# Last routing of a soft mixture of experts: logits and maximum in two parts, and a new order of the copies around them

## The chip, the core and the metric

The kernel runs on one core of a Trainium2 chip. The metric is the device time of one execution in microseconds (us). Engines are named as the profile does: PE is TensorE's matmuls and PEld its weight loads, DVE is VectorE, ACT ScalarE, POOL GpSimd, SP SyncE, which issues all the DMAs. PSUM has eight banks; the program names them 0 to 7.

## The reference

Three stages follow each other: attention in chunks of 32 queries, a dense feed-forward layer (`_moe_ref`), and a soft mixture of experts (`_moe2_ref`), in which the change lies:

```python
def _moe2_ref(x, phi, w1, w2):          # x: 3072 x 512, phi: 512 x 32 (8 experts x 4 slots)
    logits = x @ phi
    d = logits - logits.max(0, keepdims=True)
    d = np.exp(d)
    d /= d.sum(0, keepdims=True) + 1e-09
    slot_input = d.T @ x
    ...
    for e in range(E):
        h = np.maximum(slot_input[e] @ w1[e], 0.0)
        slot_out[e] = h @ w2[e]
    ...
    c = logits - logits.max(1, keepdims=True)
    c = np.exp(c)
    c /= c.sum(1, keepdims=True) + 1e-09
    return (c @ slot_out).astype(np.float32)
```

`d` is normalised over all tokens, so the slot inputs, and with them the experts, need every token. `c` is normalised over the slots of one token.

## The kernel before

The 3072 tokens go through attention and the dense layer in seven blocks (`BLOCKS`, 256 to 512 tokens). `emit_h` and `emit_y` are the dense layer's matmuls; the outputs of a block collect in PSUM as `ps_y`. `route` then does the mixture's first half for a block in steps 0 to 7: y out of PSUM, transposes of y (`ps_yt`, `yT`), logits (`ps_l`, `lp`), the logits summed over four partial groups (`ps_r`, by the 0/1 matrix `sel`), a maximum over the tokens of the block (`nm`, the negated maximum, joined with that of the blocks before), Exp (`dl`, with its sum `sb`), and from its transposes `d` the block's share of the slot inputs (`ps_a`), which is added to `acc` with the factor `al` for the changed maximum. `s_run` is the running sum. It is an online softmax over tokens.

The last block (L, 512 tokens, four y tiles) has its route written out by hand, since nothing of the dense layer is left to hide it. The code runs under a manual schedule: every engine executes its instructions in the order in which they are written, and each waits for what it reads, or for the former users of the place that it writes. For PSUM, such a wait goes by the bank. The order of the last route is (lines 666 to 716): y tile 3 out of PSUM, half by ACT and half by DVE (L666, L667); the first `c_turn`; four transposes of tile 3 (L671); the logits of 384 and of 128 tokens (L679), both behind the transposes, copied to `lp` by ACT and by DVE; a `c_turn`; the sums (L687), into one bank; `route(L, 4)` with the maximum (L427), Exp (L431), two `c_turn` and two keep-warm matmuls between, the transposes `ps_d` (L442), and a copy of 32 partitions of `ps_r` to `dl[32:64]` (L444) and `s_run` (L448); `d` (L454); a `c_turn`; the reciprocal `rs` and the normalised selector `seln` (L694 to L697); `ps_a` (L469) and `acc` (L476) in two halves; the transposes of `dl[32:64]` for the combine weights (L702); keep-warm matmuls; `ps_si`, the slot inputs (L706); a keep-warm matmul; and the copies to `siz` (L709), which the experts read.

`c_turn(t0, b, eng)` is work of another branch: four PE transposes of the combine weights of tokens 128 t0 and on into bank `b` (L501), and their copy back to `c4` by `eng` ("a" is ACT, L179; "v" is DVE, L181). Only the combine at the kernel's end reads it. `keep_warm(n, b)` is n matmuls (L175) into bank `b`, which nobody reads.

Behind it, `expert1` (L725, `ps_e`) and `expert2` (L757, `ps_o`) run over weights that SP loads in 512 KB pieces (`ew`); `to_hT` (L750) transposes the hidden rows between the two. The last `c_turn` stands behind the first `to_hT`. `slot_out` sums the slots' outputs (`ps_so`, `so`), `combine` multiplies them with the combine weights (`ps_f`, L787), copies to `ob` and writes to memory.

Of the kernel before, what the change touches and what calls it, by code (L numbers as in the profile page):

```python
# [7 lines left out]
F32 = mybir.dt.float32  # L8
# [3 lines left out]
ACTF = mybir.ActivationFunctionType  # L12
ALU = mybir.AluOpType
# [42 lines left out]
def attn_moe_softmoe_kernel(  # L56
# [12 lines left out]
    nc = tc.nc  # L69
# [312 lines left out]
    def route(j, s, between=None):  # L382
# [11 lines left out]
        elif s in (1, 2):  # L394
            y = rt[j, "y"]
            if s == 1:
                rt[j, "yT"] = st_tile(1, [128, 4, n], F32, "yT")
            yT = rt[j, "yT"]
            for c in (3,) if s == 1 else (0, 1, 2):
                pt = mbank([128, n], "ps_yt")  # L400
                for t in range(nt):
                    nc.tensor.transpose(pt[:, 128 * t:128 * t + 128], y[:, t, 128 * c:128 * c + 128], ident)  # L402
                if c % 2:
                    nc.vector.tensor_copy(out=yT[:, c], in_=pt)
                else:
                    nc.scalar.activation(out=yT[:, c], in_=pt, func=ACTF.Copy)
        elif s == 3:
            yT = rt.pop((j, "yT"))
            pl = mbank([128, n], "ps_l")
            for c in range(4):  # L410
                nc.tensor.matmul(  # L411
                    pl[32 * c:32 * c + 32], phi_sb[:, c], yT[:, c], start=True, stop=True, tile_position=(0, 32 * c)
                )
            lp = rt[j, "lp"] = [sm_p.tile([128, n], F32R, tag=tag, name=tag, bufs=1) for tag in ("lp", "ll")]
            nc.scalar.activation(out=lp[0], in_=pl, func=ACTF.Copy)
            nc.vector.tensor_tensor(out=lp[1], in0=pl, in1=lp[0].bitcast(F32), op=ALU.subtract)
        elif s == 4:
            pr = rt.pop((j, "pr"), None)
            if pr is None:
                lp = rt.pop((j, "lp"))  # L420
                pr = mbank([128, n], "ps_r")
                for m, x in enumerate(lp):
                    nc.tensor.matmul(pr, selr, x, start=(m == 0), stop=(m == len(lp) - 1))
            dl = sm_p.tile([128, n], F32, tag="lp", name="dl", bufs=1)
            sb = sm_p.tile([128, 1], F32, tag="sb", name="sb")
            nm = sm_p.tile([128, 1], F32, tag="nm", name="nm")
            nc.vector.tensor_reduce(out=nm, in_=pr, axis=AX.X, op=ALU.max, negate=True)  # L427
            if j > 0:
                al = sm_p.tile([128, 1], F32, tag="al", name="al")
                nc.vector.tensor_tensor(out=nm, in0=nm, in1=rt["nm"], op=ALU.min)  # L430
            nc.scalar.activation(out=dl, in_=pr, func=ACTF.Exp, bias=nm, accum_out=sb)  # L431
            if j > 0:
                nc.vector.tensor_tensor(out=al, in0=nm, in1=rt["nm"], op=ALU.subtract)
                nc.scalar.activation(out=al, in_=al, func=ACTF.Exp)
                rt[j, "al"] = al
            rt["nm"] = nm
            if between:
                between()
            if j == NB - 1:
                pd = mbank([128, nt, 32], "ps_d")  # L440
                for t in range(nt):
                    nc.tensor.transpose(pd[:, t], dl[0:32, 128 * t:128 * t + 128], ident[0:32, 0:32])  # L442
                rt["pd"] = pd
            nc.vector.tensor_copy(out=dl[32:64], in_=pr[32:64])  # L444
            if j == 0:
                nc.vector.tensor_copy(out=s_run, in_=sb)
            else:
                nc.vector.scalar_tensor_tensor(out=s_run, in0=s_run, scalar=al, in1=sb, op0=ALU.mult, op1=ALU.add)  # L448
            rt[j, "dl"] = dl
        elif s == 5:  # L450
            dl = rt[j, "dl"]
            d = sm_p.tile([128, nt, 32], F32, tag="d", name="d")
            if j == NB - 1:
                nc.scalar.activation(out=d, in_=rt["pd"], func=ACTF.Copy)  # L454
            else:
                pd = mbank([128, nt, 64], "ps_d")
                for t in range(nt):
                    nc.tensor.transpose(pd[:, t], dl[0:64, 128 * t:128 * t + 128], ident[0:64, 0:64])
                nc.scalar.activation(out=d, in_=pd[:, :, 0:32], func=ACTF.Copy)
                slot_scores(j, pd[:, :, 32:64])  # L460
            rt[j, "d"] = d
        elif s == 6:
            y, d = rt.pop((j, "y")), rt.pop((j, "d"))
            m = 32 * nt
            cut = (0, 256, 512) if j == NB - 1 else (0, 512)
            for lo, hi in zip(cut, cut[1:]):
                pa = mbank([128, hi - lo], "ps_a")
                for t in range(nt):
                    nc.tensor.matmul(  # L469
                        pa[32 * t:32 * t + 32], d[:, t], y[:, t, lo:hi], start=True, stop=True, tile_position=(0, 32 * t)  # L470
                    )
                if j == 0:
                    nc.vector.memset(acc, 0.0)
                    nc.vector.tensor_copy(out=acc[0:m], in_=pa[0:m])
                else:
                    nc.vector.scalar_tensor_tensor(  # L476
                        out=acc[0:m, lo:hi], in0=acc[0:m, lo:hi], scalar=rt[j, "al"][0:m], in1=pa[0:m],
                        op0=ALU.mult, op1=ALU.add,
                    )
        else:  # L480
            cs = call[:, d0:d0 + nt, :]
            cm = sm_p.tile([128, nt, 1], F32, tag="cs", name="cs")
            nc.scalar.activation(out=cs, in_=cs, func=ACTF.Exp)
            nc.vector.tensor_reduce(out=cm, in_=cs, axis=AX.X, op=ALU.add)
            nc.vector.tensor_scalar(out=cm, in0=cm, scalar1=1e-9, scalar2=None, op0=ALU.add)
            nc.vector.reciprocal(out=cm, in_=cm)
            nc.vector.tensor_tensor(out=cs, in0=cs, in1=cm.to_broadcast([128, nt, 32]), op=ALU.mult)
# [104 lines left out]
    with tc.manual_schedule():  # L592
# [72 lines left out]
        load_ew_halves(("g", {"bufs": 2}), ("gh", {}))  # L665
        nc.scalar.activation(out=y[:, 3, 0:256], in_=y_t[L][3][:, 0:256], func=ACTF.Copy, scale=0.5)  # L666
        nc.vector.tensor_scalar(out=y[:, 3, 256:512], in0=y_t[L][3][:, 256:512], scalar1=0.5, scalar2=None, op0=ALU.mult)  # L667
        c_turn(0, 0, "a")
        pt = bank(6, [128, 4, 128], "ps_yt")
        for c in range(4):  # L670
            nc.tensor.transpose(pt[:, c], y[:, 3, 128 * c:128 * c + 128], ident)  # L671
        copy("a", yT[:, 0:2, 384:512], pt[:, 0:2])
        copy("v", yT[:, 2:4, 384:512], pt[:, 2:4])
        lp = sm_p.tile([128, 512], F32, tag="lp", name="lp", bufs=1)
        parts = (slice(0, 384), slice(384, 512))
        for n, r in enumerate(parts):
            pl = bank((7, 2)[n], [128, r.stop - r.start], "ps_l")
            for c in range(4):
                nc.tensor.matmul(  # L679
                    pl[32 * c:32 * c + 32], phi_sb[:, c], yT[:, c, r], start=True, stop=True, tile_position=(0, 32 * c)  # L680
                )
            copy("av"[n], lp[:, r], pl)
        load_ew((st_p, "st1", 2))
        c_turn(4, 4, "v")
        pr = bank(3, [128, 512], "ps_r")
        for r in parts:
            nc.tensor.matmul(pr[:, r], sel, lp[:, r], start=True, stop=True)  # L687
        rt[L, "pr"], rt[L, "y"] = pr, y
        misc[0] = [5, 6, 7, 0]
        route(L, 4, lambda: (c_turn(8, 1, "v"), c_turn(12, 2, "v"), keep_warm(2, 4)))  # L690
        route(L, 5)
        c_turn(16, 4, "v")
        rs = sm_p.tile([128, 1], F32, tag="sb", name="rs")
        nc.vector.tensor_scalar(out=rs, in0=s_run, scalar1=1e-9, scalar2=None, op0=ALU.add)  # L694
        nc.vector.reciprocal(out=rs, in_=rs)
        seln = sm_p.tile([128, 32], F32, tag="d", name="seln")
        nc.vector.tensor_scalar(out=seln, in0=sel[:, 0:32], scalar1=rs, scalar2=None, op0=ALU.mult)  # L697
        route(L, 6)
        pd = mbank([128, BLOCKS[L] // 128, 32], "ps_d")
        dl = rt[L, "dl"]  # L700
        for t in range(BLOCKS[L] // 128):
            nc.tensor.transpose(pd[:, t], dl[32:64, 128 * t:128 * t + 128], ident[32:64, 32:64])  # L702
        keep_warm(2, 2)
        psi = [bank(b, [128, 2, 32], "ps_si") for b in (1, 3)]
        for c in range(4):
            nc.tensor.matmul(psi[c // 2][:, c % 2], acc[:, 128 * c:128 * c + 128], seln, start=True, stop=True)  # L706
        keep_warm(1, 2)
        for c in range(4):
            nc.vector.tensor_copy(  # L709
                out=bass.AP(  # L710
# [89 lines left out]
        pool, tag, _ = ew_free.pop(0)  # L800
        hT = pool.tile([128, 2, 8, 128], F32, tag=tag, name="hT")
        to_hT(0, hs0, hT[:, 0])
        c_turn(NT - 4, 6, "v")
        expert1(1, range(2, 4), ph1)
        hs1 = relu(1, ph1)
        po = bank(0, [128, 256], "ps_o")
# [6 lines left out]
        po1 = bank(1, [128, 256], "ps_o")  # L813
        so = slot_out(0, po, lambda: expert2(po1, 0, 1, range(2)))
        po = po1
        expert2(po, 0, 1, range(2, 3))
        for i in range(4):
            combine(0, so, i, ((0, 2), (2, 4)) if i == 0 else ((0, 4),))
# [77 lines left out]
```

## Time and profile before

| | us |
|---|---|
| device time, median of three runs | 703.95 (701.90 to 704.05) |
| device time of the profiled execution | 702.08 |
| its span, first to last instruction | 700.30 |
| PE busy in the span | 678.6 (97%) |
| DVE busy | 332.9 (48%) |
| ACT busy | 255.6 (37%) |

The rest of the profiled execution's time lies outside the span. Busy PE time counts pipelined matmuls whose ends are modelled. The part that the change touches begins at 638.3 us of the span; the experts begin at 648.85, the last output lands at the end.

### The profile page before, as it was taken

To read this page: it belongs to the slowest core of one execution; us is meant where nothing else is said; L and a number is where in the kernel's file an instruction comes from. 1 tells how busy PE (TensorE), PEld (TensorE's weight loads), DVE (VectorE), ACT (ScalarE), POOL (GpSimd) and SP (SyncE) were. 2 spreads that over 40 slices of the span, in tenths; PEclk is the share of its full clock that TensorE was granted. 3 is DMA by queue.
4 is the path that set the end of the run, shared out by engine and by line. 5 is a ranking of instruction groups with operands and counts; after the bars stand their busy time and mean duration, and the time that the engine had idled before them with its cause. 6 is when DMAs were issued, how large, how long until landed. Compare 5 with 4: busy or idle time off the path is not lost.

```text
span 700.3 us, 14761 instructions
## 1 busy us (share of the span) xinstructions
PE 678.6 (97%) x6439; PEld 545.7 (78%) x6439; DVE 332.9 (48%) x669; ACT 255.6 (37%) x474; POOL 31.7 (5%) x40
## 2 busy tenths in 40 slices
PE   4999999999999999999999999999999999999993
PEld 2899988888878887878887878887878877886352
DVE  5998977544455434433435343434432333225222
ACT  3888845333323333222333222333222232223113
POOL 0200001001000000000000000000000001000000
PEclk8899999999999999999999999999999999999998
DMA  9995012221122212102112112111002344569998
GB/s 353 402 405 207 1 37 68 71 67 60 44 68 66 67 31 66 38 31 67 37 32 66 37 32 67 37 60 38 1 31 91 120 145 165 198 207 342 401 347 271
DMA packets 27904, 85.29 MB, mean 122 GB/s; under 512 B 2624, under 2 KB 9024, under 8 KB 27840
## 3 DMA queue, kind: packets, MB, share of 16 engines
q1 hardware_dynamic: 27840, 84.36, 33.9%
q8 instruction: 50, 0.82, 0.5%
q14 instruction: 14, 0.11, 0.0%
HBM read 78.05 MB, written 6.29 MB: 120 GB/s over the span
## 4 chain that ended last, share of the span: by engine, by line
PE 95%; DMA 1%; DVE 1%; issue 1%; SPq 0%; POOL 0%; DVEq 0%; POOLq 0%
PE ps_h L336 39%; PE ps_y L366 13%; PE ps_y L367 13%; PE ps_y L370 12%; PE ps_x L305 4%; PE ps_s L239 3%; PE ps_o L757 2%; PE ps_e L725 2%; PE ps_t L287 2%; PE ps_yt L402 1%; DMA qk<-in_qk_dram 1%; PE ps_f L787 1%; PE ps_a L469 1%; PE ps_l L411 1%; PE ps_warm L175 1%
## 5 line engine op out<-in xcount | busy, mean ns | idle before, releaser
L336 PE MATMUL ps_h<-xbuf,w 128*128 128x512 f32 (+2 forms) x1344 | 287.0, 363 | 0.0
L336 PEld LDWEIGHTS ps_h<-xbuf,w 128*128 128x128 f32 x1344 | 232.2, 188 | 41.8 <-DVE gl L184 3.1
L347 DVE SCALAR_TENSOR_TENSOR g<-g,ps_h 128x512 f32<-128x512 f32 (+2 forms) x112 | 68.2, 610 | 187.1 <-ACT g L343 187.0
L366 PE MATMUL ps_y<-w,gh 128*128 128x512 f32 x384 | 150.7, 393 | 0.0
L367 PE MATMUL ps_y<-w,gh 128*128 128x512 f32 x384 | 149.9, 390 | 0.0
L343 ACT ACTIVATE g<-ps_h 128x512 f32<-128x512 f32 (+2 forms) x112 | 59.9, 535 | 193.1 <-PE ps_h L336 188.6
L370 PE MATMUL ps_y<-w,gl 128*128 128x512 f32 x384 | 106.2, 390 | 0.0
L184 DVE TENSOR_TENSOR gl<-g,gh 128x512 fp32r<-128x512 f32 (+2 forms) x112 | 68.4, 614 | 60.6 <-ACT gh L179 58.5
L179 ACT ACTIVATE gh<-g 128x512 fp32r<-128x512 f32 (+2 forms) x112 | 63.8, 570 | 70.3 <-DVE g L347 62.5
L370 PEld LDWEIGHTS ps_y<-w,gl 128*128 128x128 f32 x384 | 72.1, 188 | 15.4
L366 PEld LDWEIGHTS ps_y<-w,gh 128*128 128x128 f32 x384 | 72.1, 188 | 14.0
L367 PEld LDWEIGHTS ps_y<-w,gh 128*128 128x128 f32 x384 | 72.2, 188 | 13.7
L184 POOL TENSOR_TENSOR a<-a,smm 128x512 f32<-128x512 f32 x18 | 19.6, 1087 | 462.6 <-DVE smm L277 289.4
L247 DVE TENSOR_REDUCE mx<-ps_s 128x4 f32<-128x256 f32 x48 | 18.1, 418 | 26.7 <-PE ps_s L239 26.7
L321 DVE TENSOR_TENSOR xbuf<-ps_x,xbuf 128x256 fp32r<-128x256 f32 x48 | 17.9, 415 | 24.7 <-ACT xbuf L179 24.6
L179 ACT ACTIVATE xbuf<-ps_x 128x256 fp32r<-128x256 f32 x48 | 15.8, 381 | 30.9 <-PE ps_x L305 30.8
L305 PEld LDWEIGHTS ps_x<-at,v 64*64 64x64 f32 x1280 | 20.6, 134 | 6.8 <-issue 5.7
L269 ACT ACTIVATE a<-a 128x512 f32<-128x512 f32 x20 | 12.6, 632 | 33.1 <-DVE a L263 20.3
L305 PE MATMUL ps_x<-at,v 64*64 64x32 f32 x1280 | 22.8, 220 | 0.0
L239 PE MATMUL ps_s<-qk 64*32 64x64 f32 x1280 | 17.8, 227 | 3.0 <-issue 2.4
L205 DVE SCALAR_TENSOR_TENSOR raw<-raw 128x1024 uint32<-128x1024 uint32 (+1 forms) x17 | 20.2, 1195 | 0.2 <-ACT raw L201 0.2
L209 DVE SCALAR_TENSOR_TENSOR wx<-wx,raw 128x1024 uint32<-128x1024 uint32 (+1 forms) x17 | 20.3, 1199 | 0.0
(130 smaller groups left out, 458.1 us busy)
## 6 DMA issues: line engine op xcount, KB each, us to landing
ew<-in_w_dram SPq DMA_DIRECT2D x61, 512.0 KB, 6.1
qk<-in_qk_dram SPq DMA_DIRECT2D x20, 608.0 KB, 3.9
v<-in_v_dram SPq DMA_DIRECT2D x20, 512.0 KB, 3.6
raw<-in_wout_dram SPq DMA_DIRECT2D x16, 512.0 KB, 10.2
raw<-in_win_dram SPq DMA_DIRECT2D x16, 512.0 KB, 10.2
out_dram<-ob SPq DMA_DIRECT2D x9, 512.0 KB, 4.5
early<-in_qk_dram SPq DMA_DIRECT2D x4, 608.0 KB, 6.0
early<-in_v_dram SPq DMA_DIRECT2D x4, 512.0 KB, 10.8
```

The lines of the kernel that those rows point to most:

```text
L179: nc.scalar.activation(out=out, in_=in_, func=ACTF.Copy)
L184: (nc.gpsimd if eng == "p" else nc.vector).tensor_tensor(**kw)
L205: nc.vector.scalar_tensor_tensor(out=lo_w, in0=hi_w, scalar=0x80000000, in1=lo_w, op0=ALU.bitwise_and, op1=ALU.bitwise_or)
L209: nc.vector.scalar_tensor_tensor(out=xb, in0=xb, scalar=3, in1=lo_w, op0=ALU.logical_shift_left, op1=ALU.bitwise_or)
L239: nc.tensor.matmul(ps[r][q, p], t[h, p, q], t[h, p, w:w + 64], start=True, stop=True)
L305: nc.tensor.matmul(px[s][h, u, q], vt[k, n, c], AT[k, n, q], start=True, stop=True)
L336: nc.tensor.matmul(ph, w[:, wi, 128 * c:128 * c + 128], x[:, c, :], start=(c == 0 and m == 0), stop=(c == 3 and m == 2),)
L343: nc.scalar.activation(out=g_t[i], in_=h_t[i], func=ACTF.Tanh, scale=0.5)
L347: nc.vector.scalar_tensor_tensor(out=g, in0=g, scalar=1.0, in1=h_t.pop(i), op0=ALU.add, op1=ALU.mult)
L366: nc.tensor.matmul(y_t[j][t], gh[:, r], w[:, 0], start=(f == 0), stop=False)
L367: nc.tensor.matmul(y_t[j][t], gh[:, r], w[:, 1], start=False, stop=False)
L370: nc.tensor.matmul(y_t[j][t], gl[:, r], w[:, 0], start=False, stop=(f == NF - 1))
```

## The change

`route`'s step 4 takes a maximum that was made before (`rt[j, "nm"]`) over the first `lo` tokens, and reduces only the rest. In the last route the logits of 384 tokens come ahead of the transposes of tile 3, their sums and their maximum (`nm3`) behind these; then come the logits, sums and maximum of the other 128 tokens. The copy of these logits to `lp` is ACT's, as are the copies of four of the six `c_turn` of this stretch and behind it that were DVE's (one stays on DVE), and the copy to `dl[32:64]`, which moves behind `d`. `rs` and `seln` come ahead of `ps_a` (as a second function handed to step 4). Of five keep-warm matmuls two stay. One `c_turn` takes the place of the last keep-warm matmul ahead of the experts; the one behind the first `to_hT` goes behind the first `slot_out`. What is computed stays the same.

```diff
--- before.py
+++ after.py
@@ -424,10 +424,11 @@
             dl = sm_p.tile([128, n], F32, tag="lp", name="dl", bufs=1)
             sb = sm_p.tile([128, 1], F32, tag="sb", name="sb")
             nm = sm_p.tile([128, 1], F32, tag="nm", name="nm")
-            nc.vector.tensor_reduce(out=nm, in_=pr, axis=AX.X, op=ALU.max, negate=True)
+            first_nm, lo = rt.pop((j, "nm"), (rt.get("nm"), 0))
+            nc.vector.tensor_reduce(out=nm, in_=pr[:, lo:n], axis=AX.X, op=ALU.max, negate=True)
             if j > 0:
                 al = sm_p.tile([128, 1], F32, tag="al", name="al")
-                nc.vector.tensor_tensor(out=nm, in0=nm, in1=rt["nm"], op=ALU.min)
+                nc.vector.tensor_tensor(out=nm, in0=nm, in1=first_nm, op=ALU.min)
             nc.scalar.activation(out=dl, in_=pr, func=ACTF.Exp, bias=nm, accum_out=sb)
             if j > 0:
                 nc.vector.tensor_tensor(out=al, in0=nm, in1=rt["nm"], op=ALU.subtract)
@@ -435,23 +436,27 @@
                 rt[j, "al"] = al
             rt["nm"] = nm
             if between:
-                between()
+                between[0]()
             if j == NB - 1:
                 pd = mbank([128, nt, 32], "ps_d")
                 for t in range(nt):
                     nc.tensor.transpose(pd[:, t], dl[0:32, 128 * t:128 * t + 128], ident[0:32, 0:32])
                 rt["pd"] = pd
-            nc.vector.tensor_copy(out=dl[32:64], in_=pr[32:64])
+            else:
+                nc.vector.tensor_copy(out=dl[32:64], in_=pr[32:64])
             if j == 0:
                 nc.vector.tensor_copy(out=s_run, in_=sb)
             else:
                 nc.vector.scalar_tensor_tensor(out=s_run, in0=s_run, scalar=al, in1=sb, op0=ALU.mult, op1=ALU.add)
+            if between:
+                between[1](dl, pr)
             rt[j, "dl"] = dl
         elif s == 5:
             dl = rt[j, "dl"]
             d = sm_p.tile([128, nt, 32], F32, tag="d", name="d")
             if j == NB - 1:
                 nc.scalar.activation(out=d, in_=rt["pd"], func=ACTF.Copy)
+                nc.scalar.activation(out=dl[32:64], in_=rt.pop((j, "pl"))[32:64], func=ACTF.Copy)
             else:
                 pd = mbank([128, nt, 64], "ps_d")
                 for t in range(nt):
@@ -665,46 +670,59 @@
         load_ew_halves(("g", {"bufs": 2}), ("gh", {}))
         nc.scalar.activation(out=y[:, 3, 0:256], in_=y_t[L][3][:, 0:256], func=ACTF.Copy, scale=0.5)
         nc.vector.tensor_scalar(out=y[:, 3, 256:512], in0=y_t[L][3][:, 256:512], scalar1=0.5, scalar2=None, op0=ALU.mult)
-        c_turn(0, 0, "a")
+        lp = sm_p.tile([128, 512], F32, tag="lp", name="lp", bufs=1)
+        pr = bank(3, [128, 512], "ps_r")
+
+        def logits(r, b, eng):
+            pl = bank(b, [128, r.stop - r.start], "ps_l")
+            for c in range(4):
+                nc.tensor.matmul(
+                    pl[32 * c:32 * c + 32], phi_sb[:, c], yT[:, c, r], start=True, stop=True, tile_position=(0, 32 * c)
+                )
+            copy(eng, lp[:, r], pl)
+
+        def sums(r):
+            nc.tensor.matmul(pr[:, r], sel, lp[:, r], start=True, stop=True)
+
+        parts = (slice(0, 384), slice(384, 512))
+        logits(parts[0], 7, "a")
         pt = bank(6, [128, 4, 128], "ps_yt")
         for c in range(4):
             nc.tensor.transpose(pt[:, c], y[:, 3, 128 * c:128 * c + 128], ident)
         copy("a", yT[:, 0:2, 384:512], pt[:, 0:2])
         copy("v", yT[:, 2:4, 384:512], pt[:, 2:4])
-        lp = sm_p.tile([128, 512], F32, tag="lp", name="lp", bufs=1)
-        parts = (slice(0, 384), slice(384, 512))
-        for n, r in enumerate(parts):
-            pl = bank((7, 2)[n], [128, r.stop - r.start], "ps_l")
-            for c in range(4):
-                nc.tensor.matmul(
-                    pl[32 * c:32 * c + 32], phi_sb[:, c], yT[:, c, r], start=True, stop=True, tile_position=(0, 32 * c)
-                )
-            copy("av"[n], lp[:, r], pl)
+        sums(parts[0])
+        nm = sm_p.tile([128, 1], F32, tag="nm3", name="nm3")
+        nc.vector.tensor_reduce(out=nm, in_=pr[:, parts[0]], axis=AX.X, op=ALU.max, negate=True)
+        nc.vector.tensor_tensor(out=nm, in0=nm, in1=rt["nm"], op=ALU.min)
+        logits(parts[1], 2, "a")
+        c_turn(0, 0, "a")
+        sums(parts[1])
         load_ew((st_p, "st1", 2))
-        c_turn(4, 4, "v")
-        pr = bank(3, [128, 512], "ps_r")
-        for r in parts:
-            nc.tensor.matmul(pr[:, r], sel, lp[:, r], start=True, stop=True)
-        rt[L, "pr"], rt[L, "y"] = pr, y
+        rt[L, "pr"], rt[L, "y"], rt[L, "nm"] = pr, y, (nm, 384)
         misc[0] = [5, 6, 7, 0]
-        route(L, 4, lambda: (c_turn(8, 1, "v"), c_turn(12, 2, "v"), keep_warm(2, 4)))
+        seln = sm_p.tile([128, 32], F32, tag="d", name="seln")
+
+        def weights(dl, pr):
+            rs = sm_p.tile([128, 1], F32, tag="sb", name="rs")
+            nc.vector.tensor_scalar(out=rs, in0=s_run, scalar1=1e-9, scalar2=None, op0=ALU.add)
+            nc.vector.reciprocal(out=rs, in_=rs)
+            nc.vector.tensor_scalar(out=seln, in0=sel[:, 0:32], scalar1=rs, scalar2=None, op0=ALU.mult)
+            rt[L, "pl"] = pr
+
+        route(L, 4, (lambda: (c_turn(4, 4, "v"), c_turn(8, 1, "a"), keep_warm(1, 2)), weights))
         route(L, 5)
-        c_turn(16, 4, "v")
-        rs = sm_p.tile([128, 1], F32, tag="sb", name="rs")
-        nc.vector.tensor_scalar(out=rs, in0=s_run, scalar1=1e-9, scalar2=None, op0=ALU.add)
-        nc.vector.reciprocal(out=rs, in_=rs)
-        seln = sm_p.tile([128, 32], F32, tag="d", name="seln")
-        nc.vector.tensor_scalar(out=seln, in0=sel[:, 0:32], scalar1=rs, scalar2=None, op0=ALU.mult)
+        c_turn(12, 2, "a")
         route(L, 6)
         pd = mbank([128, BLOCKS[L] // 128, 32], "ps_d")
         dl = rt[L, "dl"]
         for t in range(BLOCKS[L] // 128):
             nc.tensor.transpose(pd[:, t], dl[32:64, 128 * t:128 * t + 128], ident[32:64, 32:64])
-        keep_warm(2, 2)
+        keep_warm(1, 4)
         psi = [bank(b, [128, 2, 32], "ps_si") for b in (1, 3)]
         for c in range(4):
             nc.tensor.matmul(psi[c // 2][:, c % 2], acc[:, 128 * c:128 * c + 128], seln, start=True, stop=True)
-        keep_warm(1, 2)
+        c_turn(16, 4, "a")
         for c in range(4):
             nc.vector.tensor_copy(
                 out=bass.AP(
@@ -800,7 +818,6 @@
         pool, tag, _ = ew_free.pop(0)
         hT = pool.tile([128, 2, 8, 128], F32, tag=tag, name="hT")
         to_hT(0, hs0, hT[:, 0])
-        c_turn(NT - 4, 6, "v")
         expert1(1, range(2, 4), ph1)
         hs1 = relu(1, ph1)
         po = bank(0, [128, 256], "ps_o")
@@ -813,6 +830,7 @@
         po1 = bank(1, [128, 256], "ps_o")
         so = slot_out(0, po, lambda: expert2(po1, 0, 1, range(2)))
         po = po1
+        c_turn(NT - 4, 0, "a")
         expert2(po, 0, 1, range(2, 3))
         for i in range(4):
             combine(0, so, i, ((0, 2), (2, 4)) if i == 0 else ((0, 4),))
```

Three engines' rows show it. First DVE, from the second `c_turn` cast (before) and the first part's maximum (now) to `acc`. `c_5830` is the tile of combine weights (`c4`), written by a `c_turn`; `nm_6585` is `nm3`. Before:

```order
L181 CAST c_5830<-ps_c 128x512
L427 TENSOR_REDUCE nm<-ps_r 128x1
L430 TENSOR_TENSOR nm<-nm 128x1
L433 TENSOR_TENSOR al<-nm 128x1
L181 CAST c_5830<-ps_c 128x512 x2
L444 COPY dl<-ps_r 32x512
L448 SCALAR_TENSOR_TENSOR s_run<-s_run,al,sb 128x1
L181 CAST c_5830<-ps_c 128x512
L694 TENSOR_SCALAR rs<-s_run 128x1
L695 RECIPROCAL rs<-rs 128x1
L697 TENSOR_SCALAR seln<-cst,rs 128x32
L476 SCALAR_TENSOR_TENSOR acc<-acc,al,ps_a 128x256 x2
```

and now:

```order
L696 TENSOR_REDUCE nm_6585<-ps_r 128x1
L697 TENSOR_TENSOR nm_6585<-nm_6585,nm 128x1
L428 TENSOR_REDUCE nm<-ps_r 128x1
L431 TENSOR_TENSOR nm<-nm,nm_6585 128x1
L434 TENSOR_TENSOR al<-nm 128x1
L181 CAST c_5830<-ps_c 128x512
L450 SCALAR_TENSOR_TENSOR s_run<-s_run,al,sb 128x1
L708 TENSOR_SCALAR rs<-s_run 128x1
L709 RECIPROCAL rs<-rs 128x1
L710 TENSOR_SCALAR seln<-cst,rs 128x32
L481 SCALAR_TENSOR_TENSOR acc<-acc,al,ps_a 128x256 x2
```

Behind the maximum stood three casts of combine weights and the copy to `dl`; now one cast is left there, and the reduction is in two rows.

Second ACT, from the first `c_turn` copy to `d`. Before:

```order
L179 ACTIVATE c_5830<-ps_c 128x512
L179 ACTIVATE yT<-ps_yt 128x2x128
L179 ACTIVATE lp<-ps_l 128x384
L431 ACTIVATE dl,sb<-ps_r,nm 128x512
L434 ACTIVATE al<-al 128x1
L454 ACTIVATE d<-ps_d 128x128
```

and now, two rows further:

```order
L179 ACTIVATE lp<-ps_l 128x384
L179 ACTIVATE yT<-ps_yt 128x2x128
L179 ACTIVATE lp<-ps_l 128x128
L179 ACTIVATE c_5830<-ps_c 128x512
L432 ACTIVATE dl,sb<-ps_r,nm 128x512
L435 ACTIVATE al<-al 128x1
L179 ACTIVATE c_5830<-ps_c 128x512
L458 ACTIVATE d<-ps_d 128x128
L459 ACTIVATE dl<-ps_r 32x512
L179 ACTIVATE c_5830<-ps_c 128x512 x2
```

The first `c_turn` copy went from ahead of the logits to right ahead of Exp; another stands between the small exponential and `d`, and behind `d` are the copy to `dl` and two more.

Third PE, from the last `ps_y` matmul to the `c_turn` transposes behind the sums. Before:

```order
L501 MATMUL ps_c<-cst,c_5830 128x128 x4
L671 MATMUL ps_yt<-cst,y 128x128 x4
L679 MATMUL ps_l<-yT,phi_sb 32x384 x4
L679 MATMUL ps_l<-yT,phi_sb 32x128 x4
L501 MATMUL ps_c<-cst,c_5830 128x128 x4
L687 MATMUL ps_r<-lp,cst 128x384
L687 MATMUL ps_r<-lp,cst 128x128
L501 MATMUL ps_c<-cst,c_5830 128x128 x8
```

and now:

```order
L679 MATMUL ps_l<-yT,phi_sb 32x384 x4
L691 MATMUL ps_yt<-cst,y 128x128 x4
L685 MATMUL ps_r<-lp,cst 128x384
L679 MATMUL ps_l<-yT,phi_sb 32x128 x4
L506 MATMUL ps_c<-cst,c_5830 128x128 x4
L685 MATMUL ps_r<-lp,cst 128x128
L506 MATMUL ps_c<-cst,c_5830 128x128 x8
```

The 384 logits took the place of the first `c_turn` transposes, which now stand behind the 128 logits; the sums of 384 tokens stand between.

## Rows read from the trace of the kernel before

**Rows 1.** Stages: length, busy PE, PEld, DVE, ACT, POOL; clock, DMA, GB/s.

```profile
643.40:649.00 5.60, 4.83 (x46) 2.78 (x48) 4.84 (x16) 1.15 (x4) 0.00 (x0) 1.00 1.03 402
660.00:670.00 10.00, 10.00 (x136) 5.24 (x138) 2.67 (x4) 1.78 (x3) 0.00 (x0) 1.00 1.03 413
678.00:684.00 6.00, 6.00 (x95) 3.35 (x94) 1.41 (x3) 1.20 (x2) 0.00 (x0) 1.00 0.84 281
687.00:690.00 3.00, 2.78 (x21) 2.41 (x19) 2.90 (x5) 2.95 (x6) 0.00 (x0) 1.00 1.03 341
```

**Rows 2.** Timeline of DVE: start, us, instruction, count [idle before <- releaser].

```profile
642.67 0.69 DVE L427 TENSOR_REDUCE nm<-ps_r 128x1 f32<-128x512 f32 x1
...
643.67 1.29 DVE L181 CAST c<-ps_c 128x512 fp32r<-128x512 f32 x2
644.99 0.68 DVE L444 COPY dl<-ps_r 32x512 f32<-32x512 f32 x1
...
645.96 0.69 DVE L181 CAST c<-ps_c 128x512 fp32r<-128x512 f32 x1
...
647.09 0.87 DVE L476 SCALAR_TENSOR_TENSOR acc<-acc,al,ps_a 128x256 f32<-128x256 f32 x2
```

**Rows 3.** Timeline of ACT, from the first copy of combine weights to d.

```profile
639.00 0.60 ACT L179 ACTIVATE c<-ps_c 128x512 fp32r<-128x512 f32 x1
...
643.67 0.69 ACT L431 ACTIVATE dl<-ps_r,nm 128x512 f32<-128x512 f32 x1 [2.50 <-DVE nm L430]
...
644.35 0.19 ACT L434 ACTIVATE al<-al 128x1 f32<-128x1 f32 x1
644.97 0.28 ACT L454 ACTIVATE d<-ps_d 128x128 f32<-128x128 f32 x1 [0.43 <-PE ps_d L442]
```

**Rows 4.** Timeline of PE, from the sums to the experts' first matmuls.

```profile
641.60 1.03 PE L687 MATMUL ps_r<-lp,cst 128*128 128x384 f32 x4
...
645.45 1.07 PE L469 MATMUL ps_a<-y,d 128*32 128x256 f32 x16
646.45 0.43 PE L702 MATMUL ps_d<-cst,dl 32*128 32x32 f32 x4
646.81 0.60 PE L175 MATMUL ps_warm<-cst 128*128 128x512 bf16 x2
647.62 1.08 PE L706 MATMUL ps_si<-seln,acc 128*128 128x32 f32 x8 [0.20 <-DVE acc L476]
648.54 0.38 PE L175 MATMUL ps_warm<-cst 128*128 128x512 bf16 x1
648.85 1.06 PE L725 MATMUL ps_e<-ew,siz 128*32 128x512 f32 x8
```

**Rows 5.** Timeline of DVE: a copy and a maximum of 128 columns.

```profile
641.22 0.29 DVE L181 COPY lp<-ps_l 128x128 f32<-128x128 f32 x1 [0.51 <-PE ps_l L679]
...
649.01 0.28 DVE L379 TENSOR_REDUCE cm<-ps_d 128x4 f32<-128x128 f32 x1
```

**Rows 6.** Timeline of PE: the last c_turn, the first ps_f, the last expert2 row.

```profile
660.22 0.60 PE L501 MATMUL ps_c<-cst,c 128*128 128x128 f32 x4
660.75 1.49 PE L725 MATMUL ps_e<-ew,siz 128*32 128x512 f32 x12
...
675.02 0.71 PE L787 MATMUL ps_f<-so,c 128*128 128x256 f32 x4 [0.50 <-DVE so L771]
...
679.38 4.52 PE L757 MATMUL ps_o<-ew,hT 128*32 128x256 f32 x80
```

**Rows 7.** SP's issues of the last weights; landing of one issued at 667.8.

```profile
646.35 21.80 SPq L512 DMA_DIRECT2D ew<-in_w_dram  x20
...
ew<-in_w_dram SPq DMA_DIRECT2D x1, 512.0 KB, 10.2
```

**Rows 8.** Two early stages, with the columns of rows 1.

```profile
5.00:10.00 5.00, 2.80 (x194) 2.11 (x192) 3.43 (x9) 1.55 (x3) 0.00 (x0) 1.00 1.01 398
10.00:25.00 15.00, 9.13 (x216) 6.64 (x216) 13.01 (x36) 9.08 (x16) 4.40 (x4) 0.66 1.03 409
```

## The prediction

> **What bounds the kernel now.** I first read the busy time by stage [rows 1]. From 660 us to 684 us TensorE has no gap, and the DMA engines are full until the weights are in. Ahead of that lies the routing of the last block. From 643.4 to 649.0 us TensorE is busy for 4.83 of 5.60 us, part of that only with keep-warm matmuls, while VectorE is busy for 4.84 of it. Nothing of the experts (L725) can start before siz, the slot inputs, so this stage is one chain, and its length is paid in full if nothing behind it takes the gain back.
>
> The order of VectorE tells what the chain waits for [rows 2]. The maximum over all 512 tokens takes 0.69 us from 642.67. Right behind it stand two casts of combine weights (1.29 us), the 32-partition copy to dl (0.68) and a third cast at 645.96 (0.69), all ahead of the running sum's reciprocal and of acc. On ScalarE [rows 3] Exp starts at 643.67, 0.31 behind the end of that maximum (643.36), after 2.50 us of idling, and d follows 1.30 later, at 644.97. On TensorE [rows 4] ps_a starts at 645.45, 0.20 after d's end, and ps_si only at 647.62, 2.17 us later, after waiting for acc, which ran 647.09 to 647.96. ps_a had left the TensorE queue by 646.45. So two things are late: the maximum, and acc behind VectorE's casts and copy. The experts begin at 648.85.
>
> **The change, part by part.**
>
> *Logits and maximum in two parts.* The logits of 384 tokens now stand ahead of the last four y transposes, where before four transposes of combine weights (c_turn 0) filled the same wait. Their inputs are there when the last ps_y matmul is out, so I cost that at nothing; if they push the y transposes back, it costs at most 0.3 us, which I keep for the range. The last 128 tokens set the time. Their logits ended just before the lp copy of 641.22 to 641.51 [rows 5], and this does not move. ScalarE makes that copy now; d has the same 128x128 shape and takes 0.28 [rows 3]. The sums of 128 tokens then run from about 641.6. All 512 columns took 1.03 us [rows 4]; a quarter of that is 0.26, half is 0.52, and I take 0.4, because the tail of the pipeline comes once whatever the length. The result stands at 642.0. The maximum over 128 columns takes 0.28, as L379 does in [rows 5], instead of 0.69: 642.3. With the same 0.31 to Exp it starts at 642.6, against 643.67. **Gain to Exp: 1.07 us**, bounds 0.8 to 1.3.
>
> The first part's maximum lies beside this. It can start when its sums are done, near 640.7, and lasts between 0.28 and 0.69, so it ends by 641.4. Both parts of ps_r are in one PSUM bank, and in the new program the second sums wait for VectorE. Behind that wait on TensorE are two sets of c_turn transposes, a keep-warm matmul and ps_d. The lp copy ends at 641.5, later than the reduction, so the wait costs nothing; if the reduction came last it would cost some 0.2.
>
> *Copies moved from VectorE to ScalarE.* Before Exp stands c_turn 0's copy. Its transposes follow the last logits and end near 641.8, and with 0.60 [rows 3] the copy is out at 642.4, before Exp at 642.6. Cover is 0.2 us; what is over that lands on Exp. Between the small exponential (ends 0.87 after Exp starts) and d stands c_turn 8's copy, again 0.60: d can start 1.3 (when nothing stands in its way) to 1.47 after Exp, and I take 1.35, since the rows of ScalarE start a little before their predecessor ends. The copy to dl[32:64] and the copies of c_turn 12 and 16 stand behind d; their readers are late transposes of ps_d, and nothing.
>
> So d starts at 643.95 and ends at 644.23, and ps_a starts at 644.43 instead of 645.45. **Gain to ps_a: 1.0 us.** The Trainium skill speaks against these moves: "Trainium Architecture — The Big Picture", The five engines, in one table, lists simple arithmetic as what ScalarE is not for, with VectorE up to about three times as fast per element. Here the rows say otherwise: a cast from PSUM of 128x512 takes 0.69 on VectorE [rows 2] and 0.60 on ScalarE [rows 3]. By the rule the sum would be that of the fourth rival below.
>
> *VectorE's queue.* Three casts and the dl copy leave its way to acc; one cast (c_turn 4) stays, behind the maximum. It ends near 644.0 even with 0.5 for its waits, and the four small steps from the running sum to the reciprocal's product take some 0.75 (from the dl copy's end at 645.67 to acc at 647.09, less 0.69 for the third cast). acc is then free at 644.8 and waits for ps_a, whose halves come 0.6 and 1.1 after its start. With 0.87 for both parts acc ends at 646.0 instead of 647.96.
>
> *ps_si.* It no longer waits for acc but for its place on TensorE: ps_a to ps_d is 1.00 (645.45 to 646.45), ps_d to the keep-warm 0.36, one keep-warm 0.22 (0.60 for two less 0.38 for one) and a handover of 0.1 [rows 4]. That is 1.68 after ps_a instead of 2.17, at 646.1. **Gain to ps_si: 1.5 us.** From ps_si to the experts were 1.23 us with one keep-warm. This becomes the four transposes of c_turn 16. Four of these cost 0.53 between ps_ht and ps_e [rows 6], 0.1 of it a handover that any change of work pays, so 0.45 instead of 0.22: **0.25 is given back**. The experts start near 647.6: gain 1.25 (0.8 to 1.5).
>
> *The last transposes of combine weights.* They go from 660.22, where TensorE has no gap, to the place ahead of the second half's third expert2 step. What goes is 0.53, less the handover of 0.1: **0.43**. At the new place TensorE waits 0.50 for so ahead of ps_f [rows 6]. They fit in by a hair; 0 to 0.1 may be lost. Their copy stands ahead of the first ob copy on ScalarE, which idles there.
>
> **Sum.** 1.07 to Exp, 1.0 to ps_a, 1.5 to ps_si, 1.25 to the experts, and 0.43 more: 1.7 us, with bounds from 1.2 to 2.3. Against the profiled execution (702.08 us, span 700.30) that is 700.4. The median of the three runs is 703.95, 1.87 us above that execution, since two of them lie near 704 and one at 701.9; against the median the sum gives **702.2 us**, 0.24% less. About 0.3%, 2.1 us here, is what a measurement of this kernel can tell from no change.
>
> *Does the rest pass it on?* The weights do not come sooner, because the DMA engines are full [rows 1]; SP's order is unchanged. The last of 20 loads is issued by 668.15 and lands about 10.2 us later, by 678.3 [rows 7], and the last matmuls of the expert2 row that ends at 683.9 [rows 6] read it. That leaves some 5 us, of which 1.7 are used. The outputs' drain starts with the outputs behind that row and has the DMA engines full from 687 to 690; before that they stand at 0.84 from 678 to 684, so the first half's outputs have room to come sooner.
>
> **Rivals.**
>
> *A larger gain.* Each bound on its good side: 1.3 to Exp, 1.5 at the experts and 0.53 instead of 0.43, or the runs falling at 702 rather than 704. For it: the stage holds 0.77 us of TensorE idling and three keep-warm matmuls go. Against it: c_turn 16 stands on the path now. Gain 2.2 to 2.5, some 701.6. Chance 0.35.
>
> *The end takes it back.* Outputs of the first half are issued while the last weights are on their way and share the engines with them, or the drain is the bound. For it: DMA at 1.03. Against it: the 5 us above. A gain of 0 to 1, 703.4. Chance 0.08.
>
> *Slower: the clock.* Three of five keep-warm matmuls go, and if TensorE's idling in the routing now lets the granted clock fall to 1.2 GHz, the experts run at half speed. The trace has one such stretch early on: TensorE was busy for 2.80 of 5 us, and from 10 to 25 us the mean granted clock is 0.66 [rows 8], which means 10.2 us at half speed and 5.1 us of lost work. Then 703.95 - 1.7 + 5.1 = 707.3. It decides only if idling rises well above 0.77 in 5.60 us, the level at which the clock stays at 1.00 [rows 1], and I expect about half of that 0.77. Chance 0.07. The Trainium skill, "TensorE: Matmul & The Clock Gate", Terms, names a monitor that watches how busy TensorE is and gates its clock; the early stretch agrees.
>
> *ScalarE three times slower than VectorE.* Copies of 2.07 us (3 x 0.69) put Exp at 643.9 and d at 646.8, 1.8 later than before; ps_si 1.3 later, the experts 1.55, with the 0.43 a loss of 1.1: 705.1. The 0.60 of [rows 3] is against it. Chance 0.02. The page named above has this rule.
>
> **How the numbers follow.** Forecast (gain 1.2 to 2.1) 0.48. Faster by over 0.3%: the larger gain, 0.35. Within 0.3%: 0.48 + 0.08 + 0.02 = 0.58. Slower: the clock, 0.07. The range leaves out the clock, and the fastest runs: from 701.9 - 2.0 = 699.9 to 703.6.
>
> **What would show it.** Exp near 642.6 and no idle gap of ScalarE over 0.3 us from there to d; ps_a near 644.4; ps_si without a wait for acc; experts near 647.6, to_hT followed at once by ps_e; ps_f no later after so. Wrong would be: d behind c_turn 8's copy by more than 0.2, a VectorE wait ahead of the second sums, a granted clock below 1.00, or ps_o waiting for a weight load.

## The result: slower by 0.75%, and not in the lines that were moved

| | before | after |
|---|---|---|
| device time, median of five runs each (us) | 703.53 (701.90 to 704.05) | 707.09 (706.54 to 709.36) |
| span of the profiled execution (us) | 700.3 | 704.8 |
| ratio after to before, 95% interval | | 1.0075 (1.006 to 1.009) |

The time lies outside the predicted range, on the slower side. The rival whose number it nearly hits, 707.3 for a clock that falls to 1.2 GHz, is not what happened. Stages of after, with the columns of [rows 1] (the first is 6.34 us later there, for a reason that follows; the last is the early stage of [rows 8]):

```profile
649.74:655.34 5.60, 5.49 (x57) 3.43 (x61) 3.56 (x16) 2.83 (x8) 0.00 (x0) 1.00 1.02 396
666.00:676.00 10.00, 10.00 (x152) 5.29 (x148) 1.41 (x3) 1.19 (x2) 0.00 (x0) 1.00 1.03 410
...
10.00:25.00 15.00, 9.72 (x236) 6.80 (x228) 13.50 (x37) 9.66 (x16) 4.88 (x5) 0.66 1.03 408
```

The granted clock is 1.00 in the routing and in the experts, that is 2.4 GHz, and 0.66 at the start as before. In the routing TensorE is busy for 5.49 of 5.60 us instead of 4.83, VectorE for 3.56 instead of 4.84: the stage did what the change is for.

**Where the time is lost.** The last `ps_y` matmul of the dense layer, ahead of everything that the diff touches, ends 6.34 us later. The chain of waits (start, us, what), before:

```profile
638.22 0.24 PE ps_y L370
638.46 0.44 PE ps_c L501 x4
```

and after:

```profile
644.57 0.24 PE ps_y L370
644.80 0.88 PE ps_l L679 x8
```

With the matmuls of the two traces matched one to one, after is 0.17 us ahead at 240 us and 0.73 behind at 300, 1.69 at 360, 3.4 at 480, 5.4 at 600. TensorE has no gap in this stretch; each pass of the dense layer just takes longer. One pass there is twelve `ps_h` steps, eight `ps_y` steps with `gh` and four with `gl`; a step is the time from one matmul's start to the next one's. In `ps_h` a piece of the weights `w` is stationary (loaded into the array first) and `xbuf`, the layer's input, streams past it; in `ps_y` a piece of `gh` or `gl`, the two parts of the hidden rows, is stationary and `w` streams. Three rows of the chain, before:

```profile
609.02 0.91 PE ps_y L370 x4
609.92 2.72 PE ps_h L336 x12
...
615.36 2.72 PE ps_h L336 x12
```

and after:

```profile
609.04 0.94 PE ps_y L370 x4
609.98 2.79 PE ps_h L336 x12
...
615.57 2.76 PE ps_h L336 x12
```

From one row of `ps_h` to the next are 5.44 us (227 ns a step) before and 5.59 (233 ns) after. From 480 to 620 us every pass that follows another directly takes 5.44 before and 5.56 to 5.60 after. Grouped by line from 480 to 620 us (busy us, mean ns of one), the matmuls are longer and the weight loads are not. Before:

```profile
L336 PE MATMUL ps_h<-xbuf,w 128*128 128x512 f32 x276 | 67.8, 394 | 0.0
L367 PE MATMUL ps_y<-w,gh 128*128 128x512 f32 x96 | 37.3, 389 | 0.0
L336 PEld LDWEIGHTS ps_h<-xbuf,w 128*128 128x128 f32 x276 | 51.0, 188 | 13.3 <-DVE gl L184 1.7 <-DVE xbuf L321 0.8
```

and after:

```profile
L336 PE MATMUL ps_h<-xbuf,w 128*128 128x512 f32 x276 | 68.6, 398 | 0.0
L367 PE MATMUL ps_y<-w,gh 128*128 128x512 f32 x92 | 36.3, 394 | 0.0
L336 PEld LDWEIGHTS ps_h<-xbuf,w 128*128 128x128 f32 x276 | 51.0, 188 | 14.6 <-issue 1.7 <-DVE smm L276 0.8 <-DVE xbuf L321 0.8
```

(The means count pipelined ends; the step is the number to go by.) These lines of the program are the same in both kernels, and so is their order. What differs is where their data stands in SBUF. The new tile `nm3` has a tag of its own in the pool `sm`, whose tags get two buffers, of 32 bytes each. The pools behind it, with `xbuf`, `g`, `gh` and `gl`, move up by these 64 bytes in each partition: in the built programs `gh` goes from 202400 to 202464, `xbuf` from 165536 to 165600. The weights `w` lie ahead of the pool and stay, from 8352. (These addresses were read from the built programs and stand in no trace. The distance does not hang on them: by the sizes of the tiles in the kernel, 131072 bytes of `w`, 20480 of the pool `st` and 5632 of `sm` lie between the starts of `w` and `xbuf`, 157184 in all, which is 614 times 256; after adds 64.)

**The stage itself** gave what the prediction says. Counted from the end of the last `ps_y` matmul (638.46, now 644.80), these rows of TensorE answer to [rows 4]:

```profile
650.80 1.07 PE L474 MATMUL ps_a<-y,d 128*32 128x256 f32 x16
...
652.39 0.97 PE L724 MATMUL ps_si<-seln,acc 128*128 128x32 f32 x8
653.20 0.63 PE L506 MATMUL ps_c<-cst,c 128*128 128x128 f32 x4
653.76 2.78 PE L743 MATMUL ps_e<-ew,siz 128*32 128x512 f32 x24
```

`ps_a` starts 6.00 us behind it instead of 6.99, `ps_si` 7.59 instead of 9.16 and without its wait for `acc`, the experts 8.96 instead of 10.39.

### The profile page after: what moved, and what is told of

It is laid out like the page before. It is cut to its first block, busy times and chain, and to the rows that moved or that the text cites. A ratio compares the mean times of both kernels' runs of the same rounds, so it can differ in the third digit from the quotient of the medians.

```text
span 704.8 us, 14758 instructions
## 1 busy us (share of the span) xinstructions
PE 684.1 (97%) x6434; PEld 544.8 (77%) x6436; DVE 330.3 (47%) x665; ACT 258.7 (37%) x480; POOL 31.7 (4%) x40
## 4 chain that ended last, share of the span: by engine, by line
PE 96%; DMA 1%; DVE 0%; issue 0%; SPq 0%; POOL 0%; ACT 0%; DVEq 0%; ACTq 0%; POOLq 0%
PE ps_h L336 39%; PE ps_y L366 13%; PE ps_y L370 13%; PE ps_y L367 13%; PE ps_x L305 4%; PE ps_s L239 2%; PE ps_o L775 2%; PE ps_e L743 2%; PE ps_t L287 2%; PE ps_yt L402 1%; DMA qk<-in_qk_dram 1%; PE ps_f L805 1%; PE ps_a L474 1%; PE ps_l L411 1%; PE ps_warm L175 1%; PE ps_r L423 0%
## 5 line engine op out<-in xcount | busy, mean ns | idle before, releaser
L366 PE MATMUL ps_y<-w,gh 128*128 128x512 f32 x384 | 152.3, 397 | 0.0
L367 PE MATMUL ps_y<-w,gh 128*128 128x512 f32 x384 | 151.8, 395 | 0.0
L370 PE MATMUL ps_y<-w,gl 128*128 128x512 f32 x384 | 108.2, 395 | 0.0
L179 ACT ACTIVATE at<-ps_t 128x512 f32<-128x512 f32 x20 | 11.9, 597 | 23.3 <-PE ps_t L287 23.3
```

The lines of the kernel that those rows point to most:

```text
L179: nc.scalar.activation(out=out, in_=in_, func=ACTF.Copy)
L366: nc.tensor.matmul(y_t[j][t], gh[:, r], w[:, 0], start=(f == 0), stop=False)
L367: nc.tensor.matmul(y_t[j][t], gh[:, r], w[:, 1], start=False, stop=False)
L370: nc.tensor.matmul(y_t[j][t], gl[:, r], w[:, 0], start=False, stop=(f == NF - 1))
```

## Experiments

Two theories stood against each other. *Place*: the loss comes from the 64 bytes, and the new order gains. *Order*: the new order itself costs, by something that the trace doesn't show. And, if it is the place: what about it.

**The change without the shift.** `nm3` goes into a tag that has room for it, so that all other tiles stand where they stood:

```diff
-        nm = sm_p.tile([128, 1], F32, tag="nm3", name="nm3")
+        nm = sm_p.tile([128, 1], F32, tag="mx", name="nm3", bufs=3)
```

> The changed kernel, with the tile nm3 in a place that the attention stage no longer uses, so that xbuf, g, gh and gl lie at the same SBUF addresses as in the kernel before (in the changed kernel they lie 64 bytes further in each partition). Theory of place: the ps_y matmuls go back from a step of 0.233 us to 0.227, the part up to the last ps_y matmul is as long as before (it ended 6.3 us later in the changed kernel), and the stage behind it keeps its gain of 1.4 + 0.4: 703.5 - 1.8 = 701.7 us, ratio 0.9975 (0.996 to 0.999). Theory of schedule (the new order itself, or the program's new instruction stream, slows the dense layer): it stays at 707, ratio 1.0075.

Measured: 700.21 us against 702.92 for before in the same runs, ratio 0.9973 (0.996 to 0.9986). The steps are back at 227 ns, and up to 600 us this kernel is level with before (0.15 us ahead). It is faster than both kernels.

**The shift without the change.** Before, with a pad of 64 bytes that nobody reads:

```diff
+        sm_p.tile([128, 16], F32, tag="pad", name="pad", bufs=1)
         siz = [g_p.tile([128, 2, 8, 32], F32, tag="gh", name="siz") for _ in range(2)]
```

> The kernel before, with nothing changed but 64 bytes per partition that are set aside ahead of xbuf, g, gh and gl and that nobody uses: the addresses of the changed kernel. Theory of place: the loss of 6.3 us ahead of the last ps_y matmul comes back without the gain of the change: 703.5 + 6.3 = 709.8, ratio 1.009 (1.006 to 1.011), with ps_y matmuls at steps of 0.233 us. Theory of schedule: 703.5, ratio 1.000.

Measured: 709.40 us, ratio 1.0095 (1.0077 to 1.0112), steps of 233 ns, and 5.6 us behind at 600 us as after is (5.4). So the place alone makes the loss and the order alone the gain; 0.95% less 0.27% is 0.68%, which lies in the interval of the 0.75% of both. *Order* has fallen.

**Other shifts.** The same pad with 128 and with 32 bytes:

> The kernel before with 128 bytes set aside instead of 64. Theory of place, if what counts is the place within 128 bytes: 703.5, ratio 1.000. If what counts is the place within 256 bytes or more, or simply any shift: as far off as with 64 bytes, ratio 1.005 to 1.011. Theory of schedule: 1.000.

> The kernel before with 32 bytes set aside. Theory of place: if what counts is whether the tiles start at 32 bytes past a multiple of 64, as all do in the kernel before and in the changed one, this one leaves that and shows something new, slower or faster; if the place within 128 bytes counts in proportion, half of the loss, ratio 1.004. Theory of schedule: 1.000.

Measured: 1.0118 (1.0098 to 1.0138) and 1.0119 (1.0102 to 1.0136). The first lies at the upper end of what was expected of any shift (1.005 to 1.011), the second far from a half loss of 1.004. The small shift costs no less than the large one, and 128 is no period.

**Which tiles, and is there a period.** A pad behind `xbuf` moves `g`, `gh`, `gl` alone by 64 bytes; a pad of 64 ahead of `xbuf` and of 192 behind it moves `xbuf` by 64 and the others by 256; and all go by 256 and by 512:

```diff
+    x_p.tile([128, 16], F32, tag="pad", name="padx", bufs=1)
```

> The kernel before, with 64 bytes set aside behind xbuf, so that only g, gh, gl and the tiles behind them move by 64 bytes; xbuf stays where it was. Theory A (each matmul's pace hangs on where its own operands stand): ps_y, which reads gh and gl, takes 233 ns a step from 240 us on, ps_h keeps 227 ns, and the time is 4 to 6 us above before. Theory B (what counts is where xbuf stands, or the two against each other): either no change at all, or a delay as large as with both moved, 6.5 us.

> The kernel before, with xbuf 64 bytes further and g, gh, gl 256 bytes further. Theory A with a period of 256 bytes: ps_y keeps 227 ns a step, ps_h takes 229 to 233, and the time is 0.5 to 2 us above before. Theory A without a period: ps_y is slow as well, and the time is 6 us or more above before. If xbuf has nothing to do with it and 256 is a period: no change.

> The kernel before with xbuf, g, gh and gl all 256 bytes further. If the place counts by its remainder at some power of two up to 256: the same time as before, steps of 227 ns. If any place other than that of before is slower, as the shifts by 32, 64 and 128 were: 6 to 9 us above before, steps of 232 to 234 ns.

> The kernel before with xbuf, g, gh and gl all 512 bytes further. With a period of 256 or 512 bytes: the same time as before. With none: 6 to 9 us above before. If 256 is slow and 512 is not, the period is 512.

Measured: `gh` and `gl` alone 1.0087 (1.0064 to 1.011), `xbuf` alone 1.0029 (1.0016 to 1.0043), 256 and 512 bytes 0.9996 (0.9981 to 1.0012) and 0.9993 (0.9979 to 1.0007). So it goes by the remainder of 256, and both kinds of tile count, `gh` and `gl` more. The chain with `gh` and `gl` moved:

```profile
609.77 0.93 PE ps_y L371 x4
610.71 2.75 PE ps_h L337 x12
...
616.25 2.75 PE ps_h L337 x12
```

and with `xbuf` moved:

```profile
610.41 0.92 PE ps_y L371 x4
611.33 2.76 PE ps_h L337 x12
...
616.87 2.76 PE ps_h L337 x12
```

The passes take 5.54 us each. Theory A, that each matmul's pace hangs on its own operands alone, has only half of it: with `gh` and `gl` moved `ps_y` is at 233 ns as expected, but `ps_h` goes from 227 to 229; with `xbuf` moved `ps_h` is at 230, but `ps_y`, whose operands stand as before by the remainder, is at 230 too. The starts of the single matmuls show how: with `gh` and `gl` moved, the first six steps of `ps_h` behind `ps_y` take 229 to 235 ns on average and the last five 227 to 228. So a slowed stretch is carried on for some steps into the next. With `xbuf` moved, `ps_y` does not settle within its twelve; why it takes longer there stays open.

**Own place, or place against the weights.** In before `w`, `xbuf`, `gh` and `gl` all have the remainder 160. A pad in the first pool moves them all by 64 bytes; the same pad with 192 more behind the small tiles moves `w` by 64 and the others by 256:

```diff
     s_run = const.tile([128, 1], F32, name="s_run")
+    const.tile([128, 16], F32, name="padc")
```

> The kernel before with the weight tiles w and everything behind them (y, the small tiles, xbuf, g, gh, gl) 64 bytes further, so that no two of these move against each other. Theory R (what counts is where the two operands of the dense layer's matmuls stand against each other, by the remainder of 256): steps of 227 ns and the time of before. Theory M (what counts is each tile's own remainder): ps_y at 233 ns, ps_h at 229 or more, 6 us above before.

> The kernel before with w and the small tiles 64 bytes further, and xbuf, g, gh, gl 256 bytes further, which by itself changed nothing. Theory R: w now stands 64 bytes off against all of them, so ps_y takes some 233 ns and the time is 5 to 9 us above before. Theory M: gh, gl and xbuf stand as before, so 227 ns and at most 2 us above before.

Measured: all moved 0.999 (0.9976 to 1.0005), `w` alone 1.0082 (1.0057 to 1.0108). The chain with all moved, and then with `w` alone moved:

```profile
609.06 2.72 PE ps_h L337 x12
...
614.50 2.72 PE ps_h L337 x12
```

```profile
609.93 0.92 PE ps_y L371 x4
610.85 2.80 PE ps_h L337 x12
...
616.41 2.80 PE ps_h L337 x12
```

With the remainder 224 for all of them the pass takes 5.44 us again, the very remainder at which `xbuf`, `gh` and `gl` were slow in after. Theory R holds: the tiles' places against each other count, not a tile's own.

**The rest of the ring.** Shifts by 96 and by 192 bytes:

> The kernel before with xbuf, g, gh and gl 96 bytes further: their remainder by 256 is 0. Theory R: slow like the shifts by 32, 64 and 128, 6 to 9 us above before. Theory M with alignment: 0 is the best of all remainders, so no slower than before.

> The kernel before with xbuf, g, gh and gl 192 bytes further, that is 64 short of a period. Theory R: slow, 5 to 9 us above before, as with 64 on the other side; were only an offset in one direction harmful, the time of before. Theory M: open, since the remainder 96 has not run.

Measured: 1.0146 (1.012 to 1.0171) and 1.0071 (1.0043 to 1.01). The shift by 96 costs 10.3 us, more than the 6 to 9 expected, and the best of all remainders by Theory M is the slowest. The shift by 192 and `w` alone by 64 put the tiles at the same distance (64 short of a period), and their passes have the same rows: 0.92 for four `ps_y`, 2.80 for twelve `ps_h`. By the distance of `xbuf`, `gh`, `gl` from `w`, modulo 256:

| distance (bytes) | ratio to before | kernels |
|---|---|---|
| 0 | 0.9993, 0.9996, 0.999 | 512, 256, all moved |
| 32 | 1.0119 | shift 32 |
| 64 | 1.0095 | shift 64 |
| 96 | 1.0146 | shift 96 |
| 128 | 1.0118 | shift 128 |
| 192 | 1.0071, 1.0082 | shift 192, `w` alone |

## Why the prediction was wrong

**The step that failed** is the sum: "Against the profiled execution (702.08 us, span 700.30) that is 700.4." It sets the gain against a span whose first 638 us it takes as unchanged. The change part by part costs every instruction that is moved, and the new tile `nm3` only as a reduction; what its two buffers do to the places of other tiles has no term. That term measured 6.3 us at the end of the dense layer, more than three times the gain. The text reads each wait of 10 us of routing, and no rival touches the 400 us ahead of it, in which after went from 0.17 us ahead to 6.34 behind: more than the routing can give. The rivals on the slower side look only at what the moved instructions do to engines and clock.

**The terms of the stage** can be judged without the shift. The chain of waits of the change with `nm3` in place (the last `ps_y` matmul ends at 638.30, 0.16 us earlier than before, which is no effect of the change):

```profile
641.94 0.30 DVE nm L428
...
642.52 0.31 ACT dl L432
...
643.78 0.59 PE ps_c L506 x4
644.37 1.00 PE ps_a L474 x16
...
646.06 0.81 PE ps_si L724 x8
646.87 0.47 PE ps_c L506 x4
647.34 10.44 PE ps_e L743 x96
657.77 1.02 PE ps_ht L768 x8
658.80 3.57 PE ps_e L743 x32
```

Against [rows 3, 4, 6], with the 0.16 taken off:

| step | predicted gain (us) | measured |
|---|---|---|
| Exp | 1.07 | 0.99 (642.52 against 643.67) |
| `ps_a` | 1.0 | 0.99 (644.30 against 645.45) |
| `ps_si` | 1.5 | 1.57 (645.89 against 647.62) |
| experts | 1.25 | 1.42 (647.27 against 648.85) |
| last `c_turn` | 0.43 | 0.44 (`ps_ht` to `ps_e`: 1.03 against 1.47) |
| its new place | 0 to -0.1 | +0.09 at the first `ps_f` (672.91 against 675.02, less the 2.02 gained by 669), 0.06 to 0.09 from there to the end |
| sum | 1.7 (1.2 to 2.3) | 1.9 |

- *Exp.* The parts are where the sum put them: the second maximum runs from 641.94 with 0.30, Exp follows at 642.52. The first part's maximum took 0.56, inside its bounds, and nobody waited for it.
- *`ps_a`.* Size and reason are right: `d` sets the start. The chain above names the transposes of `c_turn` 12 (0.59 on TensorE behind `ps_d`), but it goes by modelled ends. The weight loads show an idle gap that `d` ends, before and with `nm3` in place:

```profile
645.45 0.59 PEld L469 LDWEIGHTS ps_a<-y,d 128*32 128x32 f32 x16 [0.17 <-ACT d L454]
```

```profile
644.30 0.59 PEld L474 LDWEIGHTS ps_a<-y,d 128*32 128x32 f32 x16 [0.17 <-ACT d L458]
```

  Both start 0.20 behind `d`'s end (645.25, 644.10). The transposes are close behind, though: their last matmul starts at 644.10 and they follow each other by 0.11, so a `d` that came sooner could have gained some 0.1 more, by this estimate, and no run tried it.
- *`ps_si`* no longer waits for `acc`, as predicted; `acc` took 0.91 for both halves, where 0.87 was taken.
- *`c_turn` 16 ahead of the experts* gives back 0.15 (1.57 to 1.42), not 0.25: `ps_si` itself takes 0.97 instead of the 1.08 of [rows 4], now that no wait stands ahead of it, and the sum had no term for that.
- *ScalarE's copies.* "Trainium Architecture — The Big Picture", The five engines, in one table, in the Trainium skill, has VectorE up to three times as fast for simple arithmetic. In after the 128x512 copies take 0.59 to 0.61 on ScalarE and 0.69 on VectorE, so the fourth rival was rightly left at 0.02:

```profile
649.43 0.69 DVE L181 CAST c<-ps_c 128x512 fp32r<-128x512 f32 x1 [0.31 <-DMA ew<-in_w_dram]
...
649.79 0.59 ACT L179 ACTIVATE c<-ps_c 128x512 fp32r<-128x512 f32 x1
650.32 0.28 ACT L458 ACTIVATE d<-ps_d 128x128 f32<-128x128 f32 x1
```

- *Does the rest pass it on?* It does. With `nm3` in place the kernel is 1.6 us ahead at 660, 2.0 at 669, 2.1 at 684, and its span is 2.1 shorter (698.2): the rival by which the end takes it back has fallen.
- *The clock rival* has fallen with the granted clock of 1.00; its 707.3 and the measured 707.09 have nothing in common.

Without the shift the forecast of 0.24% less than before (702.2) stands beside 0.27% less. The mechanism of the stage was right; the kernel around it was not the same kernel.

## What to carry to other kernels

When a kernel's time is a long stream of matmuls, look at the addresses of its operands in the built program of both versions before costing the lines of a diff: a new small tile in a pool that lies ahead of them moves them all. Here it paid, over the whole kernel, to keep the two operands that TensorE reads at the same time at the same remainder of 256 bytes, and to put a new scalar into a tag that has room. When a trace of after is late at the first line that was touched, stop reading there and compare the steps of the stretch ahead.

## What was not expected of the hardware

A matmul's pace depends on where its two operands stand against each other. From 240 us on, steps of 128x512 settled at 227 ns with the moving and the stationary tiles at one remainder of 256 bytes, and took 230 to 234 on average at distances of 32, 64, 96, 128 and 192, with the same instructions, no gap of TensorE between them and the clock at 1.00. The weight load runs beside the matmul before it and kept its 188 ns.

Other engines and DMA traffic are not what each slow step meets. With `gh` and `gl` moved by 64 bytes, none of the 681 steps of `ps_y` from 240 us to the end of the dense layer is under 230 ns, and in 12 us of these (columns of [rows 1]) VectorE and ScalarE are idle for most of the time and nothing is transferred:

```profile
494.00:500.00 6.00, 6.00 (x29) 4.91 (x29) 1.77 (x5) 1.51 (x3) 0.00 (x0) 1.00 0.00 0
500.00:506.00 6.00, 6.00 (x89) 4.86 (x88) 3.25 (x9) 1.82 (x4) 0.00 (x0) 1.00 0.00 0
```

What is left fits two reads of TensorE that get in each other's way, the load for the next matmul and the stream of the present one; no run here shows that they do, and why the distance of 96 is worst, and 32 no better than 128, stays open. "SBUF — State Buffer", Who interferes with whom, in the Trainium skill, says that only the port which VectorE and GpSimd share causes contention, and its table calls TensorE's two read ports independent. In these runs only places changed, and TensorE lost 2.3 to 2.9% of its pace in the passes of after; where inside the chip, they do not tell.

One remainder alone does not give 227 ns. From 60 to 235 us of before, where `ps_h` has 256 or 384 columns, the steps of `ps_y` average 231 ns, although its operands have the same remainder there. In rows of nine matmuls behind `ps_h` they take 224 to 236 throughout; in the four rows of fifteen they are at 227 by the tenth step at the latest. So 227 is the pace to which a row settles where the places agree, and a stretch at another pace ahead of it disturbs it for some steps.

One part goes the other way. With `xbuf` alone moved by 64 bytes the kernel was 1.6 us ahead of before at 240 us, in the stretch with the smaller blocks, and lost 3.4 us from there to 660. Of the 1.6, 0.6 were there at 60 us already, and the shifts of 256 and 512, which changed no pace, are 0.8 and 0.9 ahead there; only the 1.0 from 60 to 240 can be a matter of places. So the best places seem to differ by stage, and those of before need not be the best for its first third; that was not tried.
